# One ring of large slots, small products as row vectors, and the output projection moved to the end of a decode attention kernel

## The chip, the core and the metric

The kernel runs on one core of one Trainium2 chip. The metric is device time in microseconds. Three runs of the kernel before gave 1332.81, 1330.76 and 1330.81 us, a median of 1330.81 us. Beside these stands one profiled execution, which recorded every instruction, every DMA packet and the granted clock of the matrix engine. The engines are PE (matrix products), DVE (vector), ACT (scalar functions), POOL and SP; in this kernel SP issues nearly all DMAs.

## The reference

One token is decoded. The row x has 512 elements; its layer norm is xn. The result is x + attention(xn) + MLP(xn), all in float32.

```python
q = xn @ wq                         # [512] x [512, 4096]: 32 query heads of 128
s = q_h . k_cache[h // 4] * 128 ** -0.5     # 8 key/value heads, 65536 keys of 128 each
o = softmax(s) @ v_cache[h // 4]
attention = concat(o) @ wo          # [4096] x [4096, 512]
mlp = relu(xn @ w1) @ w2            # 512 -> 1792 -> 512
```

The keys and the values are 268 MB each. wq and wo are 8.4 MB each, w1 and w2 3.7 MB each. Nothing is read twice.

## The kernel before

**Staging.** All that is read comes through SP's DMA queue, in the order of the program. Keys and values use the pool `kv`: eight buffers of 16 KB per partition, one load of 2 MB each (4096 keys, `CHUNK`). The weights use a second pool, `wpool`, of four buffers of 8 KB per partition, one load of 1 MB each. A load is issued once the buffer that it takes has been released by the last instruction that read it.

**The loop.** For each of the eight key/value heads there are 16 key chunks, then `softmax(h)`, then 16 value chunks. `score_chunk` (L157) streams 512 keys at a time through PE against the four padded queries of the head, four matmuls side by side in the four 32-column tiles of the array (L166). DVE transposes the scores in 32x32 blocks (L171), ACT copies the four used columns (L173), DVE takes a maximum per chunk (L174). `softmax` (L180) finds the maximum over all partitions and lets ACT compute the exponentials (L197). `value_chunk` (L207) streams values through PE, again in four column tiles (L213). For heads 0 to 6 a matmul is 512 columns wide and holds four 128-key blocks at once (`WIDE`), of which only the matching columns are kept; for the last head it is 128 wide (`wide`, L202).

**The small products.** They are spread over the stream. `queries(h)` (L144) makes the queries of one head at its first key chunk: the weights are the stationary operand and xn, one column, is the moving one. `mlp_in(i)` (L262) does the same with a quarter of w1. `output(h)` (L242) runs at the second key chunk of the next head: it copies the accumulator, gathers the blocks (L252), and calls `project` (L234), which multiplies with that head's part of wo. `project` cuts the 512 output columns into four pieces of 128 and puts each on a column tile of its own (L236), all adding into `acc_y`. `mlp_out(i)` does the same with w2.

**The end.** The last value loads are cut into parts (`LAST`, L29: blocks of 8, 8, 8, 8 and 8, 8, 8, 4, 4), and after them come the last two blocks of w2 (L313). Then follow `output(7)`, `mlp_out(3)`, one addition (L319) and the store of the result (L320).

The matrix engine runs each float32 matmul as two instructions, so the counts on PE in the profile are twice those of the program.

Of the kernel before, what the change touches and what calls it, by code (L numbers as in the profile page):

```python
# [14 lines left out]
P = 128  # L15
# [14 lines left out]
WIDE = 4  # L30
A = D // P
FB = DFF // P
EPS = 1e-5
# [3 lines left out]
def attention_and_mlp_kernel(  # L37
# [30 lines left out]
    xT = const.tile([P, A], F32, name="xT")  # L68
    nc.scalar.dma_start(xT, x.rearrange("(p a) -> p a", p=P))
    x4 = const.tile([P, P], F32, name="x4")  # L70

    weights = {}

    def load(name, src):
        w = wpool.tile([P, 4, 512], F32, name="w")
        n, m = src.shape[1], src.shape[2]
        nc.sync.dma_start(w[:, :n, :m], src)
        weights[name] = w

    chunks = {}  # L80

    def load_k(h, n):
        t = kv.tile([P, CHUNK], F32, name="kv")
        nc.sync.dma_start(t, k[h, n])
        chunks["k", h, n] = t

    def load_v(h, n):
        t = kv.tile([P, CHUNK], F32, name="kv")
        src = v[h, n * CHUNK : (n + 1) * CHUNK, :].rearrange("(p b) d -> p (b d)", p=P)
        b = 0  # L90
        for nb in LAST.get(n, [NB]) if h == HKV - 1 else [NB]:
            cut = slice(b * DH, (b + nb) * DH)
            nc.sync.dma_start(t[:, cut], src[:, cut])
            b += nb
        chunks["v", h, n] = t

    load(("q", 0), wq[0])

# [5 lines left out]
    # sel[32 * c + 4 * b + g, b, g] = 1  # L104
# [5 lines left out]
    nc.vector.memset(x4, 0.0)  # L110
    qpad = [const.tile([P, 32], F32, name=f"qpad{i}") for i in range(2)]
    for t in qpad:
        nc.vector.memset(t, 0.0)
# [4 lines left out]
    nc.vector.memset(acc_y[:, :P], 0.0)  # L118

# [17 lines left out]
    # A Newton step: r * (1.5 - 0.5 * v * r * r).  # L137
# [6 lines left out]
    def queries(h):  # L144
        w = weights.pop(("q", h))
        pq = ps_m.tile([P, 512], F32, name="pm")
        for g in range(G):
            for a in range(A):
# [4 lines left out]
        nc.vector.tensor_copy(qpad[h % 2][:, :G], pq[:, :G])  # L153

    scores, chunk_max, probs, part_sum = {}, {}, {}, {}

    def score_chunk(h, n):  # L157
        t = chunks.pop(("k", h, n))
        if n == 0:
            scores[h] = work.tile([P, NCH * NB, G], F32, name="scores")  # L160
            chunk_max[h] = work.tile([P, G, NCH], F32, name="chunk_max")
        for s in range(TPC):
            pt = ps_s.tile([P, TW], F32, name="pt")
            for c in range(CT):
                lo = (s * CT + c) * TW
                nc.tensor.matmul(  # L166
                    pt[32 * c : 32 * c + 32, :], qpad[h % 2], t[:, lo : lo + TW],
                    start=True, stop=True,
                )
# [3 lines left out]
            nc.scalar.copy(scores[h][:, b0 : b0 + SUB, :], tr[:, :, :G])  # L173
        nc.vector.reduce_max(  # L174
            chunk_max[h][:, :, n],
            scores[h][:, n * NB : (n + 1) * NB, :].rearrange("p b g -> p g b"),
            axis=AX.X,
        )

    def softmax(h):  # L180
        m = work.tile([P, G], F32, name="m")
        nc.vector.reduce_max(m, chunk_max.pop(h), axis=AX.X)  # L182
# [10 lines left out]
        probs[h] = work.tile([P, NCH * NB, G], F32, name="probs")  # L193
        part_sum[h] = work.tile([P, G], F32, name="part_sum")
        s = scores.pop(h)
        for g in range(G):
            nc.scalar.activation(  # L197
                probs[h][:, :, g], s[:, :, g], AF.Exp, bias=bias[:, g : g + 1], scale=scale,
                accum_out=part_sum[h][:, g : g + 1],
            )  # L200

    def wide(h):  # L202
        """128-key blocks of one matmul: the columns of each meet the weights of all, and the
        block's own are kept. One for the last head, whose output is wanted soon."""
        return 1 if h == HKV - 1 else WIDE

    def value_chunk(h, n):  # L207
        t = chunks.pop(("v", h, n))
        w = wide(h)
        for i in range(NB // w):  # L210
            c = i % CT
            b = n * NB + i * w
            nc.tensor.matmul(  # L213
                acc_o[h % 2][32 * c : 32 * c + w * G, : w * DH],
                probs[h][:, b : b + w, :].rearrange("p b g -> p (b g)"),
                t[:, i * w * DH : (i + 1) * w * DH],
                start=(n == 0 and i < CT), stop=(n == NCH - 1 and i >= NB // w - CT),
            )

    norm = {}  # L220

    def totals(h):
        """1 / sum of a head's weights, in the places that gather its column tiles."""
        pm = ps_m.tile([P, 512], F32, name="pm")
        nc.tensor.matmul(pm[:, :G], ones, part_sum.pop(h), start=True, stop=True)  # L225
        r = work.tile([P, G], F32, name="r")
        nc.vector.reciprocal(r, pm[:, :G])  # L227
        norm[h] = work.tile([P, WIDE, G], F32, name="norm")
        for b in range(wide(h)):
            nc.vector.tensor_mul(norm[h][:, b, :], sel[:, b, :], r)  # L230
# [3 lines left out]
    def project(lhsT, row, last=False):  # L234
        for c in range(CT):
            nc.tensor.matmul(  # L236
                acc_y[32 * c : 32 * c + 1, :P], lhsT, row[:, c * P : (c + 1) * P],
                start=first[0], stop=last,
            )
        first[0] = False  # L240

    def output(h):  # L242
        probs.pop(h)
        n = wide(h)
        o = work.tile([P, WIDE, DH], F32, name="o")
        nc.vector.tensor_copy(  # L246
            o[:, :n, :].rearrange("p b d -> p (b d)"), acc_o[h % 2][:, : n * DH]
        )
        r = norm.pop(h)
        pm = ps_m.tile([P, 512], F32, name="pm")  # L250
        for b in range(n):
            nc.tensor.matmul(pm[:, :G], o[:, b, :], r[:, b, :], start=(b == 0), stop=(b == n - 1))  # L252
        oT = work.tile([P, G], F32, name="oT")
        nc.vector.tensor_copy(oT, pm[:, :G])  # L254
        w = weights.pop(("o", h))
        for g in range(G):
            project(oT[:, g : g + 1], w[:, g, :])

    hT = const.tile([P, FB], F32, name="hT")
    FQ = 4  # parts that the MLP's weights come in  # L260

    def mlp_in(i):  # L262
        w = weights.pop(("1", i))
        n = min(4, FB - 4 * i)
        pm = ps_m.tile([P, 512], F32, name="pm")
        for j in range(n):
            for a in range(A):
                nc.tensor.matmul(  # L268
                    pm[:, j : j + 1], w[:, a, j * P : (j + 1) * P], xn[:, a : a + 1],
                    start=(a == 0), stop=(a == A - 1),  # L270
                )
        nc.vector.tensor_scalar_max(hT[:, 4 * i : 4 * i + n], pm[:, :n], 0.0)

    def mlp_out(i):
        w = weights.pop(("2", i))
        for b in range(4 * i, min(4 * i + 4, FB)):
            project(hT[:, b : b + 1], w[:, b - 4 * i, :], last=(b == FB - 1))

# [1 line left out]
    for h in range(HKV):  # L280
        for n in range(NCH):
            load_k(h, n)
            if n == 0:
                queries(h)
            if n == 1:
                if h == 0:
# [63 lines left out]
```

## Time and profile before

| | |
|---|---|
| median of three runs | 1330.81 us (1330.76 to 1332.81) |
| span of the profiled execution | 1329.9 us |
| read from HBM | 560.99 MB, 422 GB/s over the span |
| PE busy | 795.2 us (60%) |
| DVE busy | 255.2 us (19%) |
| ACT busy | 103.5 us (8%) |
| keys in PE, L166 | 354.2 us in 2048 instructions |
| values in PE, L213 | 354.1 us in 2816 instructions |
| output and MLP projection, L236 | 14.5 us (with oT) |

The profiled execution is 0.9 us shorter than the median of the runs by its span; no other time of it is recorded. In the rows that are quoted below, a line such as `L166 PE MATMUL pt<-kv,qpad` reads: line 166 of the kernel, engine, operation, result and operands by the program's names. The two numbers after the bar are the busy time in us and the mean of one in ns; after the second bar stands the idle time of the engine before these instructions, and what ended most of it. "DMA share" is the busy share of the core's 16 DMA engines. A packet is the piece that one DMA engine moves as one; in this kernel it is one partition's row of a load.

### The profile page before, as it was taken

The numbers are of one execution on the slowest core, as the hardware profiler recorded it, in microseconds if no ns is written. First come the engines' busy times: TensorE is split into PE (matmuls) and PEld (weight loads), VectorE is DVE, ScalarE is ACT, GpSimd is POOL, SyncE is SP. The second block draws the span as 40 slices with busy tenths as digits, with TensorE's granted clock in tenths as the row PEclk, the third lists the DMA queues.
The fourth block names the chain that finished last, engine by engine and source line by source line (L and its number), as shares of the span: only waits on it lengthen the run. The fifth ranks groups of instructions, "written<-read, shape, count | busy, mean of one in ns | idle before, by whom it ended". The sixth has DMA issues, their size and how long they took to land.

```text
span 1329.9 us, 13199 instructions
## 1 busy us (share of the span) xinstructions
PE 795.2 (60%) x5702; PEld 241.1 (18%) x5702; DVE 255.2 (19%) x504; ACT 103.5 (8%) x323; POOL 0.7 (0%) x6
## 2 busy tenths in 40 slices
PE   5646757466555576655665456655666565665555
PEld 3211212112121121111211101111021110221233
DVE  3330023300233002330023300232003320033200
ACT  1020000200001000011000200002000120001100
POOL 0000000000000000000000000000000000000000
PEclk9777687777887767767777787776777867777777
DMA  9999999999999999999999999999999999999996
GB/s 394 427 429 426 427 423 428 428 426 428 425 428 427 427 427 426 426 427 427 427 429 427 428 427 428 426 429 429 426 427 429 425 429 428 426 428 428 426 426 274
DMA packets 43226, 561.86 MB, mean 422 GB/s; under 512 B 4760, under 2 KB 5280, under 8 KB 8224
## 3 DMA queue, kind: packets, MB, share of 16 engines
q1 hardware_dynamic: 43024, 561.01, 99.5%
q8 instruction: 45, 0.74, 0.2%
q14 instruction: 13, 0.11, 0.0%
q10 hardware_dynamic: 144, 0.00, 0.0%
HBM read 560.99 MB, written 0.00 MB: 422 GB/s over the span
## 4 chain that ended last, share of the span: by engine, by line
DMA 91%; PE 6%; ACT 2%; DVE 1%; issue 0%; SPq 0%; ACTq 0%
DMA kv<-k 47%; DMA kv<-v 41%; PE pt L166 3%; DMA w<-wo 3%; PE acc_o L213 2%; ACT probs L197 1%; PE acc_y L236 0%; DVE tr L171 0%; PE pm L225 0%; PE pm L252 0%; PE pm L190 0%; DVE chunk_max L174 0%; DVE mg L186 0%; PE pm L184 0%; ACT scores L173 0%
## 5 line engine op out<-in xcount | busy, mean ns | idle before, releaser
L166 PE MATMUL pt<-kv,qpad 128*32 128x512 f32 x2048 | 354.2, 823 | 240.5 <-DMA kv<-k 221.1
L213 PE MATMUL acc_o<-kv,probs 128*16 128x512 f32 (+1 forms) x2816 | 354.1, 655 | 209.1 <-DMA kv<-v 209.0
L171 DVE STREAM_TRANSPOSE tr<-pt 128x512 f32<-128x512 f32 x256 | 183.2, 716 | 347.2 <-PE pt L166 340.0
L166 PEld LDWEIGHTS pt<-kv,qpad 128*32 128x32 f32 x2048 | 78.5, 131 | 493.1 <-issue 282.8
L213 PEld LDWEIGHTS acc_o<-kv,probs 128*16 128x16 f32 (+1 forms) x2816 | 80.5, 110 | 462.9 <-DMA kv<-v 327.5
L173 ACT COPY scores<-tr 128x64 f32<-128x64 f32 x256 | 62.3, 243 | 1121.5 <-DVE tr L171 1121.5
L153 DVE COPY qpad<-pm 128x4 f32<-128x4 f32 x8 | 1.3, 162 | 376.4 <-PE pm L149 376.4
L174 DVE TENSOR_REDUCE chunk_max<-scores 128x4 f32<-128x128 f32 x128 | 48.5, 379 | 39.0 <-ACT scores L173 39.0
L246 DVE COPY o<-acc_o 128x512 f32<-128x512 f32 (+1 forms) x8 | 5.1, 642 | 225.7 <-PE acc_o L213 225.7
L149 PE MATMUL pm<-xn,w 128*128 128x1 f32 x256 | 40.0, 291 | 4.4 <-DMA w<-wq 2.6
L149 PEld LDWEIGHTS pm<-xn,w 128*128 128x128 f32 x256 | 39.5, 247 | 12.9 <-issue 11.1
L197 ACT ACTIVATE probs<-scores,bias 128x512 f32<-128x512 f32 x32 | 37.7, 1180 | 16.4 <-DVE bias L192 16.4
L225 PE MATMUL pm<-part_sum,ones 128*128 128x4 f32 x16 | 4.7, 365 | 42.4 <-ACT probs L197 42.4
L236 PE MATMUL acc_y<-w,oT 128*1 128x128 f32 x256 | 14.5, 331 | 2.0 <-DVE oT L254 2.0
L268 PEld LDWEIGHTS pm<-xn,w 128*128 128x128 f32 x112 | 14.5, 212 | 5.3 <-DMA w<-w 5.3
L268 PE MATMUL pm<-xn,w 128*128 128x1 f32 x112 | 14.9, 266 | 0.6 <-DMA w<-w 0.6
L252 PE MATMUL pm<-norm,o 128*128 128x4 f32 x58 | 8.8, 273 | 6.1 <-DVE o L246 6.1
L225 PEld LDWEIGHTS pm<-part_sum,ones 128*128 128x128 f32 x16 | 4.0, 312 | 43.1 <-ACT probs L197 43.1
L236 PEld LDWEIGHTS acc_y<-w,oT 128*1 128x1 f32 x256 | 9.3, 100 | 10.1 <-issue 5.6
L252 PEld LDWEIGHTS pm<-norm,o 128*128 128x128 f32 x58 | 8.1, 214 | 15.7 <-DVE o L246 15.7
L184 PE MATMUL pm<-ident,m 128*4 128x128 f32 x8 | 2.3, 284 | 14.3 <-DVE m L182 14.3
L227 DVE RECIPROCAL r<-pm 128x4 f32<-128x4 f32 x8 | 1.5, 183 | 45.9 <-PE pm L225 45.9
(47 smaller groups left out, 41.7 us busy)
## 6 DMA issues: line engine op xcount, KB each, us to landing
kv<-k SPq DMA_DIRECT2D x128, 2048.0 KB, 36.3
kv<-v SPq DMA_DIRECT2D x126, 2048.0 KB, 36.7
w<-wq SPq DMA_DIRECT2D x8, 1024.0 KB, 34.3
w<-wo SPq DMA_DIRECT2D x8, 1024.0 KB, 35.7
w<-w SPq DMA_DIRECT2D x6, 1024.0 KB, 36.7
kv<-v SPq DMA_DIRECT2D x7, 512.0 KB, 29.4
w<-w SPq DMA_DIRECT2D x1, 512.0 KB
kv<-v SPq DMA_DIRECT2D x2, 256.0 KB, 9.1
```

What stands on the lines that cost most here:

```text
L149: nc.tensor.matmul(pq[:, g : g + 1], w[:, a, g * DH : (g + 1) * DH], xn[:, a : a + 1], start=(a == 0), stop=(a == A - 1),)
L166: nc.tensor.matmul(pt[32 * c : 32 * c + 32, :], qpad[h % 2], t[:, lo : lo + TW], start=True, stop=True,)
L171: nc.vector.transpose(tr.rearrange("p b i -> p (b i)"), pt)
L173: nc.scalar.copy(scores[h][:, b0 : b0 + SUB, :], tr[:, :, :G])
L174: nc.vector.reduce_max(chunk_max[h][:, :, n], scores[h][:, n * NB : (n + 1) * NB, :].rearrange("p b g -> p g b"), axis=AX.X,)
L197: nc.scalar.activation(probs[h][:, :, g], s[:, :, g], AF.Exp, bias=bias[:, g : g + 1], scale=scale, accum_out=part_sum[h][:, g : g + 1],)
L213: nc.tensor.matmul(acc_o[h % 2][32 * c : 32 * c + w * G, : w * DH], probs[h][:, b : b + w, :].rearrange("p b g -> p (b g)"), t[:, i * w * ...
L225: nc.tensor.matmul(pm[:, :G], ones, part_sum.pop(h), start=True, stop=True)
L236: nc.tensor.matmul(acc_y[32 * c : 32 * c + 1, :P], lhsT, row[:, c * P : (c + 1) * P], start=first[0], stop=last,)
L246: nc.vector.tensor_copy(o[:, :n, :].rearrange("p b d -> p (b d)"), acc_o[h % 2][:, : n * DH])
L252: nc.tensor.matmul(pm[:, :G], o[:, b, :], r[:, b, :], start=(b == 0), stop=(b == n - 1))
L268: nc.tensor.matmul(pm[:, j : j + 1], w[:, a, j * P : (j + 1) * P], xn[:, a : a + 1], start=(a == 0), stop=(a == A - 1),)
```

## The change

There is now one pool, `ring`, of five slots of 32 KB per partition, for everything that is read. Key and value loads are 4 MB (8192 keys, 64 blocks of 128). wq is read first, in two loads of 4 MB, and the queries of all heads are made before the first key. w1 and w2 are read after the first head's values, one load each. wo is read last, after the last value, in parts of 8192, 4096, 2048, 1024, 512 and 512 columns, that is 4, 2, 1, 0.5, 0.25 and 0.25 MB.

The products with wq and w1 now have xn as the stationary operand, one column, and stream the weights, 512 columns at a time in four column tiles (`columns`); four transposes bring the row back onto partitions. `project` no longer uses four column tiles of 128 columns: it is one matmul of 512 columns into row 0 of `acc_y`. `output(h)` only gathers a head's output into `oT`; the 32 projections with wo, one per query head, all stand at the end behind `output(7)`. The last head's values use the 512-wide form as well, and its loads are no longer cut. The pool `work` has one buffer instead of two for most tiles.

```diff
-CHUNK = 4096  # keys of one load
+CHUNK = 8192
-LAST = {NCH - 2: [8, 8, 8, 8], NCH - 1: [8, 8, 8, 4, 4]}  # the blocks of the last loads, in parts
+LAST = [HALF * 2048, HALF * 2048 // 2, 2048, 1024, 512, 512]
...
-    kv = ctx.enter_context(tc.tile_pool(name="kv", bufs=8))
-    wpool = ctx.enter_context(tc.tile_pool(name="wpool", bufs=4))
-    work = ctx.enter_context(tc.tile_pool(name="work", bufs=2))
+    ring = ctx.enter_context(tc.tile_pool(name="ring", bufs=5))
+    work = ctx.enter_context(tc.tile_pool(name="work", bufs=1))
...
+    tq = [load_wq(i) for i in range(2)]
...
-    def queries(h):
...
+    def columns(weights, widths, relu=False):
+        pr = ps_m.tile([P, 512], F32, name="pm")
+        nc.vector.memset(pr, 0.0)
+        for a in range(A):
+            for c, n in enumerate(widths):
                 nc.tensor.matmul(
-                    pq[:, g : g + 1], w[:, a, g * DH : (g + 1) * DH], xn[:, a : a + 1],
+                    pr[32 * c : 32 * c + 1, :n], xn[:, a : a + 1], weights(c, a),
                     start=(a == 0), stop=(a == A - 1),
                 )
...
+        pt = ps_m.tile([P, 512], F32, name="pm")
+        for j in range(4):
+            nc.tensor.transpose(pt[:, j * P : (j + 1) * P], rows[:, j * P : (j + 1) * P], ident)
...
     def project(lhsT, row, last=False):
-        for c in range(CT):
-            nc.tensor.matmul(
-                acc_y[32 * c : 32 * c + 1, :P], lhsT, row[:, c * P : (c + 1) * P],
-                start=first[0], stop=last,
-            )
+        nc.tensor.matmul(acc_y[0:1, :], lhsT, row, start=first[0], stop=last)
...
+        if h == 0:
+            mlp(*load_mlp())
...
+    output(HKV - 1, norm)
+    for row, n, t in parts:
+        for f in range(row, row + n, D):
+            hg = f // D
+            project(oT[:, hg : hg + 1], t[:, f % ROW : f % ROW + D], last=(hg == HQ - 1))
-    y = const.tile([P, P], F32, name="y")
-    nc.vector.tensor_add(y, acc_y[:, :P], x4)
-    nc.sync.dma_start(out.rearrange("(c n) -> c n", c=CT), y[0:P:32, :])
+    y = const.tile([1, D], F32, name="y")
+    nc.vector.tensor_add(y, acc_y[0:1, :], x1)
+    nc.sync.dma_start(out.rearrange("(o n) -> o n", o=1), y)
```

In the built program PE executes, at the end, the last value matmuls, the four of `output(7)`, and then the 32 projections in the order of wo's parts.

More of the change, by code (lines that the diff above doesn't have):

```diff
@@ L69, in attention_and_mlp_kernel, with slot, load_wq @@
     nc.scalar.dma_start(xT, x.rearrange("(p a) -> p a", p=P))
[L70 to L80, printed above, removed]
+    x1 = const.tile([1, D], F32, name="x1")
+    def slot():
+        return ring.tile([P, ROW], F32, name="slot")
+    def load_wq(i):
+        t = slot()
+        nc.sync.dma_start(
+            t.rearrange("p (h f) -> p h f", h=HALF),
+            wq[i * HALF : (i + 1) * HALF].rearrange("h p a f -> p h (a f)"),
+        )
+        return t
     def load_k(h, n):
-        t = kv.tile([P, CHUNK], F32, name="kv")
+        t = slot()
         nc.sync.dma_start(t, k[h, n])
-        chunks["k", h, n] = t
+        return t
     def load_v(h, n):
-        t = kv.tile([P, CHUNK], F32, name="kv")
+        t = slot()
         src = v[h, n * CHUNK : (n + 1) * CHUNK, :].rearrange("(p b) d -> p (b d)", p=P)
[L90 to L97, printed above, removed]
+        nc.sync.dma_start(t, src)
+        return t
+    tq = [load_wq(i) for i in range(2)]
+    nc.scalar.dma_start(x1, x.rearrange("(o n) -> o n", o=1))
     ident = const.tile([P, P], F32, name="ident")
@@ L109, in attention_and_mlp_kernel @@
     nc.vector.tensor_add(sel, sel, places[3])
[L110 to L113, printed above, removed]
+    qall = const.tile([P, HKV, 32], F32, name="qall")
+    nc.vector.memset(qall, 0.0)
     acc_o = [ps_a.tile([P, 512], F32, name=f"acc_o{i}") for i in range(2)]
@@ L142, in attention_and_mlp_kernel, with score_chunk @@
     nc.vector.tensor_scalar_mul(xn, xc, st[:, 7:8])
-    def queries(h):
[L145 to L148, printed above, removed]
+    def columns(weights, widths, relu=False):
[3 more added lines that the diff above has]
+            for c, n in enumerate(widths):
                 nc.tensor.matmul(
-                    pq[:, g : g + 1], w[:, a, g * DH : (g + 1) * DH], xn[:, a : a + 1],
+                    pr[32 * c : 32 * c + 1, :n], xn[:, a : a + 1], weights(c, a),
                     start=(a == 0), stop=(a == A - 1),
                 )
[L153 to L161, printed above, removed]
+        rows = work.tile([P, 512], F32, name="rows")
+        if relu:
+            nc.vector.tensor_scalar_max(rows, pr, 0.0)
+        else:
+            nc.vector.tensor_copy(rows, pr)
+        pt = ps_m.tile([P, 512], F32, name="pm")
+        for j in range(4):
+            nc.tensor.transpose(pt[:, j * P : (j + 1) * P], rows[:, j * P : (j + 1) * P], ident)
+        return pt.rearrange("p (j c l) -> p c j l", j=4, c=CT)[:, :, :, 0]
+    for i, t in enumerate(tq):
+        w = t.rearrange("p (h a f) -> p h a f", h=HALF, a=A)
+        nc.vector.tensor_copy(
+            qall[:, i * HALF : (i + 1) * HALF, :G], columns(lambda c, a: w[:, c, a, :], [512] * 4)
+        )
+    scores = chunk_max = probs = part_sum = norm = None
+    def score_chunk(h, n, t):
         for s in range(TPC):
@@ L166, in score_chunk @@
                 nc.tensor.matmul(
-                    pt[32 * c : 32 * c + 32, :], qpad[h % 2], t[:, lo : lo + TW],
+                    pt[32 * c : 32 * c + 32, :], qall[:, h, :], t[:, lo : lo + TW],
                     start=True, stop=True,
@@ L192, in softmax @@
         nc.vector.tensor_copy(bias, pb[:, :G])
-        probs[h] = work.tile([P, NCH * NB, G], F32, name="probs")
-        part_sum[h] = work.tile([P, G], F32, name="part_sum")
-        s = scores.pop(h)
         for g in range(G):
             nc.scalar.activation(
-                probs[h][:, :, g], s[:, :, g], AF.Exp, bias=bias[:, g : g + 1], scale=scale,
-                accum_out=part_sum[h][:, g : g + 1],
-            )
[L202 to L210, printed above, removed]
+                probs[:, :, g], scores[:, :, g], AF.Exp, bias=bias[:, g : g + 1], scale=scale,
@@ L211, in value_chunk @@
+                accum_out=part_sum[:, g : g + 1],
+            )
+    def value_chunk(h, n, t):
+        for i in range(NB // WIDE):
             c = i % CT
-            b = n * NB + i * w
+            b = n * NB + i * WIDE
             nc.tensor.matmul(
[L214 to L217, printed above, removed]
-            )
@@ L220, in attention_and_mlp_kernel, with totals @@
-    norm = {}
-    def totals(h):
+                acc_o[h % 2][32 * c : 32 * c + WIDE * G, :],
+                probs[:, b : b + WIDE, :].rearrange("p b g -> p (b g)"),
+                t[:, i * 512 : (i + 1) * 512],
+                start=(n == 0 and i < CT), stop=(n == NCH - 1 and i >= NB // WIDE - CT),
+            )
+    def totals():
         pm = ps_m.tile([P, 512], F32, name="pm")
-        nc.tensor.matmul(pm[:, :G], ones, part_sum.pop(h), start=True, stop=True)
+        nc.tensor.matmul(pm[:, :G], ones, part_sum, start=True, stop=True)
@@ L226, in totals, with output @@
         r = work.tile([P, G], F32, name="r")
         nc.vector.reciprocal(r, pm[:, :G])
-        norm[h] = work.tile([P, WIDE, G], F32, name="norm")
-        for b in range(wide(h)):
-            nc.vector.tensor_mul(norm[h][:, b, :], sel[:, b, :], r)
+        t = work.tile([P, WIDE, G], F32, name="norm", bufs=2)
+        for b in range(WIDE):
+            nc.vector.tensor_mul(t[:, b, :], sel[:, b, :], r)
+        return t
+    oT = const.tile([P, HQ], F32, name="oT")
+    def output(h, norm):
+        o = work.tile([P, WIDE, DH], F32, name="o")
+        nc.vector.tensor_copy(o.rearrange("p b d -> p (b d)"), acc_o[h % 2])
+        pm = ps_m.tile([P, 512], F32, name="pm")
+        for b in range(WIDE):
+            nc.tensor.matmul(pm[:, :G], o[:, b, :], norm[:, b, :], start=(b == 0), stop=(b == WIDE - 1))
+        nc.vector.tensor_copy(oT[:, h * G : (h + 1) * G], pm[:, :G])
@@ L259, in attention_and_mlp_kernel @@
[L259 to L270, printed above, removed]
-                )
-        nc.vector.tensor_scalar_max(hT[:, 4 * i : 4 * i + n], pm[:, :n], 0.0)
@@ L316, in attention_and_mlp_kernel, with load_mlp @@
-    output(HKV - 1)
-    mlp_out(FQ - 1)
-    y = const.tile([P, P], F32, name="y")
-    nc.vector.tensor_add(y, acc_y[:, :P], x4)
-    nc.sync.dma_start(out.rearrange("(c n) -> c n", c=CT), y[0:P:32, :])
+        nc.tensor.matmul(acc_y[0:1, :], lhsT, row, start=first[0], stop=last)
+        first[0] = False
+    hT = const.tile([P, 4 * CT], F32, name="hT")
+    def load_mlp():
+        t1, t2 = slot(), slot()
+        nc.sync.dma_start(t1[:, : A * DFF], w1.rearrange("p a f -> p (a f)"))
+        nc.sync.dma_start(t2[:, : FB * D], w2.rearrange("p j n -> p (j n)"))
+        return t1, t2
@@ new lines, in mlp @@
+    def mlp(t1, t2):
+        w = t1[:, : A * DFF].rearrange("p (a f) -> p a f", a=A)
+        ends = [min(DFF, 512 * (c + 1)) for c in range(CT)]
+        nc.vector.tensor_copy(
+            hT.rearrange("p (c j) -> p c j", c=CT),
+            columns(
+                lambda c, a: w[:, a, 512 * c : ends[c]],
+                [ends[c] - 512 * c for c in range(CT)], relu=True,
+            ),
+        )
+        for j in range(FB):
+            project(hT[:, j : j + 1], t2[:, j * D : (j + 1) * D])
@@ new lines, in attention_and_mlp_kernel @@
+    for h in range(HKV):
+        scores = work.tile([P, NCH * NB, G], F32, name="scores")
+        chunk_max = work.tile([P, G, NCH], F32, name="chunk_max")
+        probs = work.tile([P, NCH * NB, G], F32, name="probs")
+        part_sum = work.tile([P, G], F32, name="part_sum")
+        for n in range(NCH):
+            t = load_k(h, n)
+            if n == 1 and h > 0:
+                output(h - 1, norm)
+            score_chunk(h, n, t)
+        softmax()
+        for n in range(NCH):
+            t = load_v(h, n)
+            if n == 0:
+                norm = totals()
+            value_chunk(h, n, t)
+        if h == 0:
+            mlp(*load_mlp())
@@ new lines, in attention_and_mlp_kernel @@
+    row, parts = 0, []
+    for n in LAST:
+        if (row * n) % ROW == 0 and row % ROW == 0:
+            t = slot()
+        parts.append((row, n, t))
+        while n:
+            h, f = divmod(row, 2048)
+            m = min(n, 2048 - f)
+            if n >= 2048 and f == 0:
+                m = n - n % 2048
+                nc.sync.dma_start(
+                    t[:, row % ROW : row % ROW + m].rearrange("p (h f) -> p h f", f=2048),
+                    wo[h : h + m // 2048].rearrange("h p g f -> p h (g f)"),
+                )
+            else:
+                nc.sync.dma_start(
+                    t[:, row % ROW : row % ROW + m], wo[h].rearrange("p g f -> p (g f)")[:, f : f + m]
+                )
+            row += m
+            n -= m
```

66 lines of the change are left out of this document (7 added, 59 removed).

## The prediction

> **What bounds the kernel now.** I read the page first: engines, slices, DMA, the chain.
>
> ```profile
> span 1329.9 us, 13199 instructions
> PE 795.2 (60%) x5702; PEld 241.1 (18%) x5702; DVE 255.2 (19%) x504; ACT 103.5 (8%) x323; POOL 0.7 (0%) x6
> ...
> DMA  9999999999999999999999999999999999999996
> GB/s 394 427 429 426 427 423 428 428 426 428 425 428 427 427 427 426 426 427 427 427 429 427 428 427 428 426 429 429 426 427 429 425 429 428 426 428 428 426 426 274
> ...
> HBM read 560.99 MB, written 0.00 MB: 422 GB/s over the span
> ...
> DMA 91%; PE 6%; ACT 2%; DVE 1%; issue 0%; SPq 0%; ACTq 0%
> ...
> L246 DVE COPY o<-acc_o 128x512 f32<-128x512 f32 (+1 forms) x8 | 5.1, 642 | 225.7 <-PE acc_o L213 225.7
> ```
>
> The DMA engines are busy in every slice but the last, at about 427 GB/s, while PE is busy 60%: the kernel is as long as its reading, plus the start and the end. All bytes are still read once, so only three things can move the time: how fast the bytes come, what precedes the first, and what follows the last. The timeline of the end, and the DMA view of 1320 to 1323 us (40 slices of 75 ns):
>
> ```profile
> 1320.88 1.90 PE L213 MATMUL acc_o<-kv,probs 128*4 128x128 f32 x32 [0.65 <-DMA kv<-v]
> ...
> 1322.86 0.29 DVE L246 COPY o<-acc_o 128x128 f32<-128x128 f32 x1 [70.73 <-PE acc_o L213]
> ...
> 1324.04 1.89 PE L236 MATMUL acc_y<-w,oT 128*1 128x128 f32 x32 [0.26 <-DVE oT L254]
> ...
> 1325.70 1.08 PE L236 MATMUL acc_y<-w,hT 128*1 128x128 f32 x16
> 1326.85 0.29 DVE L319 TENSOR_TENSOR y<-acc_y,x 128x128 f32<-128x128 f32 x1 [2.86 <-PE acc_y L236]
> 1327.17 0.60 SPq L320 DMA_DIRECT2D y<-y  x1
> ```
>
> ```profile
> GB/s 191 219 218 137 219 218 191 219 218 218 191 164 164 191 219 191 219 218 191 191 164 164 137 109 109 55 109 109 109 109 109 109 109 109 109 82 82 82 27 0
> ```
>
> The last byte lands at 1322.9 us, and 7.0 us follow it, of which the store takes 2.7 (1327.17 to 1329.9). The small remaining projections take 2.8 us.
>
> **Part 1: larger packets.** The DMA view of a stretch with 16 KB packets only, and of one with a load of w1, whose rows are 2 KB:
>
> ```profile
> DMA packets 2348, 34.23 MB, mean 428 GB/s; under 512 B 259, under 2 KB 259, under 8 KB 259
> ...
> q1 hardware_dynamic: 2346, 34.19, 100.5%
> ```
>
> ```profile
> DMA packets 626, 2.39 MB, mean 399 GB/s; under 512 B 32, under 2 KB 32, under 8 KB 544
> ...
> q1 hardware_dynamic: 626, 2.39, 99.8%
> ```
>
> The first is 840 to 920 us. Without the 259 tiny packets, 2087 packets of 16 KB use 80 us x 16 engines x 1.005, that is 0.616 us each. The second is 28.5 to 34.5 us: 512 packets of 2 KB and 82 of 16 KB use 6 x 16 x 0.998 = 95.8 us; less 82 x 0.616, a 2 KB packet takes 0.0885. Eight of them are 0.708 against 0.616, so a packet costs (0.708 - 0.616) / 7 = 0.013 us beside its bytes. A share above 100% says that packets of an engine overlap a little; I take off 0.5% of 0.616, which leaves 0.010 us. If a 32 KB row is one packet, the 128 key and value loads have 16384 packets fewer: 16384 x 0.010 / 16 engines = 10.2 us. w1 and w2 have 2048 + 640 packets by the code before and 256 rows of 28 KB after, some 2430 fewer, 1.5 us. Together -11.7 us. The bounds: 0 if a row is still moved 16 KB at a time (the trace shows no longer packet), -15 at 0.013; a loss has no row for it, since the rate only rises with the row. I take the fitted value, the nearest. The last byte then lands at 1311.2.
>
> **Part 2: the projection at the end.** This part sets the sign. After the last value byte come 8.4 MB of wo, 20 us. In this time PE does the last value chunk (16 matmuls, at most 7.3 us by the rows below) and `output(7)` (1.2 us from the copy at 1322.86 to the projections at 1324.04, some 0.4 more with a wide copy). That is over before the first 4 MB of wo have landed, which is 10 us before the last byte (4.2 MB at 427 GB/s, 9.8 us). From there 32 projections of 512 columns follow, each two instructions, all on one column tile. Their price is read from the timeline at two granted clocks, with the weight loads of each group of four tiles:
>
> ```profile
> 39.27 3.64 PE L166 MATMUL pt<-kv,qpad 128*32 128x512 f32 x16 [1.43 <-DMA kv<-k]
> 40.09 0.23 PEld L166 LDWEIGHTS pt<-kv,qpad 128*32 128x32 f32 x4 [0.62 <-issue]
> 40.94 0.23 PEld L166 LDWEIGHTS pt<-kv,qpad 128*32 128x32 f32 x4 [0.62 <-issue]
> ...
> 49.06 1.92 PE L166 MATMUL pt<-kv,qpad 128*32 128x512 f32 x16 [1.29 <-DMA kv<-k]
> 49.49 0.15 PEld L166 LDWEIGHTS pt<-kv,qpad 128*32 128x32 f32 x4 [0.27 <-DVE chunk_max L174]
> 49.92 0.16 PEld L166 LDWEIGHTS pt<-kv,qpad 128*32 128x32 f32 x4 [0.27 <-issue]
> ```
>
> ```profile
> 39.20:43.00 3.80, 3.64 (x16) 0.69 (x16) 0.75 (x2) 0.24 (x1) 0.00 (x0) 0.50 0.99 423
> 49.00:51.00 2.00, 1.92 (x16) 0.50 (x16) 0.96 (x2) 0.07 (x1) 0.00 (x0) 1.00 0.96 410
> 1320.80:1329.90 9.10, 5.23 (x82) 2.84 (x82) 0.74 (x3) 0.00 (x0) 0.00 (x0) 0.50 0.09 34
> ```
>
> The column after POOL is the granted clock. At 1.00 a group of four follows the other by 0.43 us, at 0.50 by 0.85: exactly the ratio of the clocks. Weights load meanwhile, so they cost nothing. In such a group each tile streams its own 512 columns, so I price a lone matmul of 512 columns like the whole group: 0.43 us an instruction. So four tiles in company do four times the work of one alone, and a single tile gives that up: 32 x 2 x 0.427 = 27.3 us at full clock, where four tiles of 128 would need 6.8. The bounds are 0.107 us an instruction (tiles share one stream; 6.8 us in all) and 0.85 (half clock; 54.6 us). The last row shows that PE ends at clock 0.50 before, although it worked 5.2 of 9.1 us; and from 39.2 on it stayed at 0.50 through 3.6 us of dense work. I take 4.2 us at half clock before it rises, 2.1 us more (an estimate, somewhat over those 3.6).
>
> The Trainium skill (TensorE: Matmul & The Clock Gate, Part 3) measures 3.07 times the speed of one tile for four row tiles, not 4. By that a lone instruction would take 0.33 us, the projections 21.0, and the sum below would be 6.3 less, 1329. The groups show a full 512 columns per tile and clock, so I stay with the row.
>
> The end, counted from the last byte: start -10.0; 27.3 + 2.1 of projections; 0.2 until DVE starts; 0.7 for an addition now 512 wide (L246's mean, 642 ns, on as many columns); 2.7 for the store. That is +23.0 against +7.0 before: +16.0 us. The wait that ends last is no longer for a DMA but for PE, which works through landed slots.
>
> **Part 3: what is hidden.** The first keys, in the timeline:
>
> ```profile
> 17.28 6.83 PE L166 MATMUL pt<-kv,qpad 128*32 128x512 f32 x48 [0.26 <-DVE qpad L153]
> ```
>
> A slot of 4 MB takes 9.8 us to arrive and at most 2 x 3.64 = 7.3 us of PE, so slots come free in time, and five slots hold 49 us of reading against eight buffers of 4.9 us before. What hides all small work is this queue:
> - wq first: the keys' first matmul moves from 17.3 us (row above) to some 31, when key chunk 0 lands after 12.6 MB. The first wq slot is free at about 19 us, and the queue is filled to 49. Cost 0; without that cover it would be some 14 us.
> - w1 and w2: `columns` takes 16 matmuls (7 us at half clock), a copy like L246's and four transposes, the 14 projections of w2 12 to 24 us. This delays the next head's keys by up to 24 us after w2 has landed, and four slots of 9.8 us stand behind it. Cost 0.
> - `softmax` and single buffers in `work`: the chain is the same, and scores, exponentials and values of one head already follow each other on PE. Cost 0. The gathering of `output(h)` now stands ahead of the next keys, about 2 us of PE waiting on DVE, inside the 2.5 us of slack per slot. Cost 0.
> - SP issues some 140 loads instead of 280; each waits for a slot, and nothing but loads stands behind it. Cost 0.
> - The start: the first load is issued as before. Cost 0.
>
> **The sum.** 1329.9 - 11.7 + 16.0 = 1334.2 for the profiled execution. Its span is 0.9 below the median of the runs, so 1330.8 + 4.3 = 1335.1 us: slower by 0.3%, just over the 0.2% (2.7 us) that a measurement of this kernel can tell from no change.
>
> **The rivals.**
> - *The clock doesn't rise at the end.* One tile of four and one column of 32 may not count as work for what grants the clock. Then the projections take 54.6 us in place of 29.4: 1360. For it: the clock of 0.50 in the last row. Against it: with PE working only in stretches of 2 to 4 us, the clock was 0.50 at 39.2 and 1.00 at 49.0 us, and here are 27 us without a pause. The Trainium skill (TensorE: Matmul & The Clock Gate, Part 1) has the clock doubled after some 3.4 us of sustained work and says nothing of lone tiles; by it this rival falls and 1335 stands.
> - *A lone tile streams faster than one of four* (ends on the other side). If an instruction took half, 0.213 us, the projections would end 13.6 us earlier: 1321, faster. It decides from 4.3 / 64 = 0.067 us less, at 0.36 us an instruction. For it: no row shows a lone tile. Against it: the groups scale exactly with the clock, not with shared reading. A milder form, company costing a tile a quarter of its speed (0.33 us an instruction, 21 us in all), ends at 1329, no change.
> - *Packets stay at 16 KB*, so part 1 doesn't do what it says: 10.2 us more, 1345. For it: no longer packet in the trace. Against it: none is asked for there.
>
> **How the numbers follow.** The forecast, 1331 to 1341 (gain of part 1 from 5 to 15, cold clock from 0 to 4 us): 0.55, of which 0.10 lies within 0.2%. Clock stays low: 0.20. Lone tile faster: 0.15, of which 0.05 at 1329. Packets of 16 KB: 0.10. So faster 0.11 (0.10 of the lone tile, 0.01 of the forecast), same 0.15, slower 0.74. To leave out no more than 0.2 the range must take in the low clock: 1328 to 1361.
>
> **What would show it.** Right: GB/s in the middle slices near 430; packets of 32 KB, half as many; the last byte near 1311; 64 instructions on the projection's line spaced 0.43 us, from about 1301 to 1331, at clock 1.00 after some 4 us; the chain ending in PE, not DMA. Wrong: 427 GB/s in the middle (part 1), spacing of 0.85 or 0.21 us (part 2), idle DMA near 180 to 220 us, where the MLP now stands (part 3).

## The result, and the profile after

The changed kernel takes 1336.63 us (median of four runs, 1336.1 to 1337.29) against 1331.13 us for the kernel before on the same chip (the three runs above and a fourth, 1331.46 us): 1.0041 times as long, with a 95% interval of 1.0026 to 1.0055. It is slower by 5.5 us. The profiled execution has a span of 1334.3 us, 4.4 more than before.

The page of the kernel after, in the parts that answer to those shown of before:

```profile
span 1334.3 us, 10207 instructions
PE 788.5 (59%) x4404; PEld 192.4 (14%) x4404; DVE 248.7 (19%) x437; ACT 103.5 (8%) x323; POOL 0.7 (0%) x6
...
GB/s 393 440 424 439 424 435 429 431 431 426 436 428 434 430 429 435 427 434 429 427 433 430 431 433 428 434 427 435 428 430 434 425 438 424 438 425 431 433 419 84
DMA packets 21344, 561.64 MB, mean 421 GB/s; under 512 B 2354, under 2 KB 2354, under 8 KB 2740
...
DMA 81%; PE 16%; ACT 2%; DVE 1%; issue 0%; SPq 0%; DVEq 0%; ACTq 0%
DMA slot<-k 50%; DMA slot<-v 27%; PE pt L177 7%; PE acc_o L216 6%; DMA slot<-wo 3%; PE acc_y L247 2%; ACT probs L205 2%; DVE tr L182 0%; DVE chunk_max L185 0%; PE pm L226 0%; PE pm L201 0%; DVE mg L197 0%; PE pm L195 0%; ACT scores L184 0%; DVE dg L199 0%
...
L247 PE MATMUL acc_y<-slot,oT 128*1 128x512 f32 x64 | 29.2, 619 | 3.1 <-DMA slot<-wo 3.1
```

The middle slices move about 431 GB/s in place of 427, with half the packets. The last slice moves 84 GB/s in place of 274: the reading ends early, and something else fills the rest. PE is no busier over the whole span (59%). Its share of the chain that ended last rose from 6 to 16%, but that alone says little of the end: the projection (L247) has only 2% of it, and the key and value matmuls (L177, L216) have 13%. The sign is that the projection's line is busy for 29.2 us in one piece. The timeline of the end:

```profile
1292.23 5.01 PE L216 MATMUL acc_o<-slot,probs 128*16 128x512 f32 x32 [3.30 <-DMA slot<-v]
...
1299.16 0.16 DVE L242 COPY oT<-pm 128x4 f32<-128x4 f32 x1 [1.15 <-PE pm L241]
...
1302.18 29.17 PE L247 MATMUL acc_y<-slot,oT 128*1 128x512 f32 x64 [3.06 <-DMA slot<-wo]
1302.99 0.13 PEld L247 LDWEIGHTS acc_y<-slot,oT 128*1 128x1 f32 x1 [0.72 <-issue]
1303.84 0.13 PEld L247 LDWEIGHTS acc_y<-slot,oT 128*1 128x1 f32 x1 [0.72 <-issue]
...
1305.87 0.08 PEld L247 LDWEIGHTS acc_y<-slot,oT 128*1 128x1 f32 x1 [0.34 <-issue]
1306.30 0.09 PEld L247 LDWEIGHTS acc_y<-slot,oT 128*1 128x1 f32 x1 [0.34 <-issue]
...
1331.39 0.68 DVE L318 TENSOR_TENSOR y<-acc_y,x 1x512 f32<-1x512 f32 x1 [32.07 <-PE acc_y L247]
1332.10 0.33 SPq L319 DMA_DIRECT2D y<-y  x1
```

PE waits until 1302.18 for the first 4 MB of wo, and then works through 64 instructions without a pause, first 0.85 and then 0.43 us apart. The stretches show why (the column after POOL is the granted clock), and the DMA view of 1305 to 1320 us (40 slices of 0.375 us) shows when the reading ended:

```profile
1302.20:1305.40 3.20, 3.20 (x4) 0.45 (x5) 0.00 (x0) 0.00 (x0) 0.00 (x0) 0.51 0.89 362
1305.50:1331.30 25.80, 25.80 (x61) 4.91 (x59) 0.00 (x0) 0.00 (x0) 0.00 (x0) 1.00 0.11 42
```

```profile
GB/s 339 306 213 197 208 284 219 202 240 224 191 197 197 158 33 55 49 38 0 0 0 0 0 0 0 0 0 0 0 0 0 0 0 0 0 0 0 0 0 0
```

The clock rose after 3.2 us of lone-tile work. The last byte landed at 1311.7. So the kernel has both at once: 11.2 us less reading than before (1322.9 to 1311.7), and 22.6 us behind the last byte in place of 7.0.

### The profile page after: what moved, and what is told of

The parts are those of the page before. It is cut to its first block, busy times and chain, and to the rows that moved or that the text cites. A ratio compares the mean times of both kernels' runs of the same rounds, so it can differ in the third digit from the quotient of the medians.

```text
span 1334.3 us, 10207 instructions
## 1 busy us (share of the span) xinstructions
PE 788.5 (59%) x4404; PEld 192.4 (14%) x4404; DVE 248.7 (19%) x437; ACT 103.5 (8%) x323; POOL 0.7 (0%) x6
## 2 busy tenths in 40 slices
DMA packets 21344, 561.64 MB, mean 421 GB/s; under 512 B 2354, under 2 KB 2354, under 8 KB 2740
## 4 chain that ended last, share of the span: by engine, by line
DMA 81%; PE 16%; ACT 2%; DVE 1%; issue 0%; SPq 0%; DVEq 0%; ACTq 0%
DMA slot<-k 50%; DMA slot<-v 27%; PE pt L177 7%; PE acc_o L216 6%; DMA slot<-wo 3%; PE acc_y L247 2%; ACT probs L205 2%; DVE tr L182 0%; DVE chunk_max L185 0%; PE pm L226 0%; PE pm L201 0%; DVE mg L197 0%; PE pm L195 0%; ACT scores L184 0%; DVE dg L199 0%
## 5 line engine op out<-in xcount | busy, mean ns | idle before, releaser
L177 PE MATMUL pt<-slot,qall 128*32 128x512 f32 x2048 | 361.3, 868 | 243.4 <-DMA slot<-k 243.4
L216 PE MATMUL acc_o<-slot,probs 128*16 128x512 f32 x2048 | 347.4, 844 | 206.8 <-DMA slot<-v 206.8
L177 PEld LDWEIGHTS pt<-slot,qall 128*32 128x32 f32 x2048 | 95.5, 151 | 502.5 <-issue 496.5
L216 PEld LDWEIGHTS acc_o<-slot,probs 128*16 128x16 f32 x2048 | 68.2, 125 | 478.4 <-DMA slot<-v 257.2
L238 DVE COPY o<-acc_o 128x512 f32<-128x512 f32 x8 | 5.5, 692 | 549.1 <-PE acc_o L216 549.1
L185 DVE TENSOR_REDUCE chunk_max<-scores 128x4 f32<-128x256 f32 x64 | 38.5, 602 | 19.8 <-ACT scores L184 19.8
L205 ACT ACTIVATE probs<-scores,bias 128x512 f32<-128x512 f32 x32 | 37.7, 1184 | 18.2 <-DVE bias L203 18.2
L247 PE MATMUL acc_y<-slot,oT 128*1 128x512 f32 x64 | 29.2, 619 | 3.1 <-DMA slot<-wo 3.1
L150 PE MATMUL pm<-slot,xn 128*1 128x512 f32 (+1 forms) x96 | 17.8, 888 | 12.7 <-DMA slot<-wq 10.4
L247 PE MATMUL acc_y<-slot,hT 128*1 128x512 f32 x28 | 12.2, 592 | 0.9 <-DMA slot<-w 0.9
L247 PEld LDWEIGHTS acc_y<-slot,oT 128*1 128x1 f32 x64 | 5.4, 86 | 25.9 <-issue 22.8
```

The costliest lines, as they stand in the source:

```text
L150: nc.tensor.matmul(pr[32 * c : 32 * c + 1, :n], xn[:, a : a + 1], weights(c, a), start=(a == 0), stop=(a == A - 1),)
L177: nc.tensor.matmul(pt[32 * c : 32 * c + 32, :], qall[:, h, :], t[:, lo : lo + TW], start=True, stop=True,)
L185: nc.vector.reduce_max(chunk_max[:, :, n], scores[:, n * NB : (n + 1) * NB, :].rearrange("p b g -> p g b"), axis=AX.X,)
L205: nc.scalar.activation(probs[:, :, g], scores[:, :, g], AF.Exp, bias=bias[:, g : g + 1], scale=scale, accum_out=part_sum[:, g : g + 1],)
L216: nc.tensor.matmul(acc_o[h % 2][32 * c : 32 * c + WIDE * G, :], probs[:, b : b + WIDE, :].rearrange("p b g -> p (b g)"), t[:, i * 512 : (i ...
L238: nc.vector.tensor_copy(o.rearrange("p b d -> p (b d)"), acc_o[h % 2])
```

## The experiments

The theory: larger packets save some 11 us, and the projection on one column tile, which nothing covers at the end, costs some 16. Each part can be had without the other. All runs are compared with the 1336.6 us of the changed kernel or with the kernel before, which was run again beside each group of them and took 1330.8 to 1331.5 us; the groups ran on different chips.

**Four tiles, nothing else.** The changed kernel with the old form of the projection (the addition and the store go back to four rows with it):

```diff
-        nc.tensor.matmul(acc_y[0:1, :], lhsT, row, start=first[0], stop=last)
+        for c in range(4):
+            nc.tensor.matmul(
+                acc_y[32 * c : 32 * c + 1, :128], lhsT, row[:, c * 128 : (c + 1) * 128],
+                start=first[0], stop=last,
+            )
```

> The changed kernel with the old form of the projection: four matmuls of 128 columns on four column tiles, nothing else. My theory (a lone column tile gives up a factor of four, and the end waits for PE): the 32 projections need 6.8 us at full clock in place of 29.2, so they keep up with the landing of wo and end within 0.5 us of the last byte at 1311.7. Behind it 0.2 + 0.3 (a narrower addition) + 2.7 us: a span of about 1315.3, 19 us less than the 1334.3 of the changed kernel; 1318 by the clock of the runs, 1.0% faster than the kernel before. Rival (the end is held by the landing of wo's parts or by the clock at half speed, not by the form of the matmul): less than 5 us gained, 1332 or more.

Measured: 1318.48 us (1318.3 to 1318.88), 0.9904 times the kernel before (0.9887 to 0.9920); a span of 1316.8. Its timeline at the end:

```profile
1302.38 8.55 PE L250 MATMUL acc_y<-slot,oT 128*1 128x128 f32 x224 [2.78 <-DMA slot<-wo]
...
1311.23 0.96 PE L250 MATMUL acc_y<-slot,oT 128*1 128x128 f32 x21 [0.31 <-DMA slot<-wo]
...
1313.19 0.60 PE L250 MATMUL acc_y<-slot,oT 128*1 128x128 f32 x11 [1.00 <-issue]
...
1313.83 0.29 DVE L324 TENSOR_TENSOR y<-acc_y,x 128x128 f32<-128x128 f32 x1 [14.03 <-PE acc_y L250]
```

Of the 32 projections, 28 (224 instructions) are done in 8.55 us, and PE waits for wo's last parts again. This form alone gives back 18.2 us. It beats both kernels, by 1.4% and 1.0%. The span is 1.5 us over the expected one; 1.0 of that is the idle time before 1313.19. The row names no wait for it, but the packed trace has the last semaphore increment of a wo load at 1312.8 us, inside this time, so most of it looks like a wait for the last part. The clock was slow for longer here than in the changed kernel:

```profile
1302.40:1307.00 4.60, 4.60 (x88) 3.15 (x92) 0.00 (x0) 0.00 (x0) 0.00 (x0) 0.50 0.79 321
```

**Two tiles.** The same with two matmuls of 256 columns, on two column tiles:

```diff
-        nc.tensor.matmul(acc_y[0:1, :], lhsT, row, start=first[0], stop=last)
+        for c in range(2):
+            nc.tensor.matmul(
+                acc_y[64 * c : 64 * c + 1, :256], lhsT, row[:, c * 256 : (c + 1) * 256],
+                start=first[0], stop=last,
+            )
```

> The changed kernel with the projection cut into two matmuls of 256 columns on two column tiles. If the cost is that of columns per tile, the projections take 13.7 us at full clock and 1.7 for the cold start: from 1302.2 to 1317.5, then 0.2 + 0.4 + 2.7; a span of 1320.9, 13.4 less than the changed kernel, 1323 by the runs. If tiles in company slow each other (3.07 for four), two would gain less than half: 1325 or more.

Measured: 1323.34 us (1322.99 to 1323.8), a span of 1321.2. In its timeline the projection is one row:

```profile
1302.37 15.67 PE L250 MATMUL acc_y<-slot,oT 128*1 128x256 f32 x128 [2.75 <-DMA slot<-wo]
```

15.67 us on two tiles, 29.17 on one; without the slow first stretch (some 1.6 us in each) it is 14.1 against 27.6, half. So two tiles in company are not slower than one alone, and the price that was read from groups of four was not too high for a lone tile.

**Half of the lone-tile work under cover.** The form stays, but the first 4 MB of wo are read before the last head's values, and their 16 projections stand there:

```diff
         softmax()
+        if h == HKV - 1:
+            early = slot()
+            nc.sync.dma_start(
+                early.rearrange("p (h f) -> p h f", f=2048),
+                wo[0:HALF].rearrange("h p g f -> p h (g f)"),
+            )
...
+            if h == HKV - 1 and n == 1:
+                for hg in range(HALF * G):
+                    project(oT[:, hg : hg + 1], early[:, hg * D : (hg + 1) * D])
...
-    row, parts = 0, []
-    for n in LAST:
+    row, parts = HALF * 2048, []
+    for n in LAST[1:]:
```

> The changed kernel with the lone-tile projection as it is, but the first half of wo (4 MB) is read before the last head's values and its 16 projections stand there, under the reading; 16 are left for the end. My theory (the loss is work on a lone tile that nothing covers): 16 projections from the landing of the next 2 MB, 4.9 us before the last byte at 1311.7, that is 1306.8 + 13.7 + 1.7 for the cold start + 0.2 + 0.7 + 2.7: a span of 1325.8, 8.5 us less than the changed kernel, 1328 by the runs. Rival (the end is set by the landing and the store, or the 16 early ones are not hidden): 1334 or more.

Measured: 1328.03 us (ten runs, 1326.96 to 1328.49), a span of 1326.1; 0.9978 times the kernel before (0.9968 to 0.9987). Two rows of its timeline, one for the early and one for the late work:

```profile
1228.52 14.35 PE L247 MATMUL acc_y<-slot,oT 128*1 128x512 f32 x29
...
1310.11 13.04 PE L247 MATMUL acc_y<-slot,oT 128*1 128x512 f32 x30
```

The line of the DMA view of 1220 to 1260 us, around the early work:

```profile
DMA packets 636, 17.29 MB, mean 432 GB/s; under 512 B 65, under 2 KB 65, under 8 KB 65
```

The same 14 us cost nothing at 1228, where the reading went on at 432 GB/s, while at 1310 most of it lies bare behind the last byte. So the place matters as much as the form. That the slow form is free was seen here and in the MLP of the changed kernel; other places were not tried. The 1328 us were met partly by luck: the late projections began at 1308.1 in place of 1306.8 us, because PE was still busy with the last values, and the 1.7 us of slow clock were not paid, because the clock had risen at 1307.1 under those values.

**Rows of 16 and of 8 KB.** The changed kernel, each key and value load in two or in four DMAs:

```diff
-        nc.sync.dma_start(t, k[h, n])
+        for i in range(2):
+            nc.sync.dma_start(t[:, i * 4096 : (i + 1) * 4096], k[h, n][:, i * 4096 : (i + 1) * 4096])
...
-        nc.sync.dma_start(t, src)
+        for i in range(2):
+            nc.sync.dma_start(t[:, i * 4096 : (i + 1) * 4096], src[:, i * 4096 : (i + 1) * 4096])
```

> The changed kernel with each key and value load cut in two DMAs with rows of 16 KB in place of 32 KB; slots, order and compute unchanged. My theory (a packet costs 0.010 us beside its bytes): 16384 packets more, 10.2 us more of reading, 427 GB/s in the middle in place of 431, a span of 1344.5 and 1347 by the runs. Rival (the shorter reading came from the small weights, from fewer loads or from the ring): at most 1.5 us more, 1338.

> The changed kernel with each key and value load cut in four DMAs with rows of 8 KB. If the cost is one of each packet (0.010 us, as 16 KB rows gave 10.6 us in all): 49152 packets more than with 32 KB, 31 us, 418 GB/s in the middle and 1368 by the runs. If it were a cost of rows above 16 KB or of the number of loads alone, under 1358.

Measured: 1347.28 us (1346.98 to 1348.49) and 1369.13 us (two runs, 1368.41 and 1369.84). The line of packets in the DMA view of 840 to 920 us, for the changed kernel, for 16 KB and for 8 KB:

```profile
DMA packets 1187, 34.45 MB, mean 431 GB/s; under 512 B 134, under 2 KB 134, under 8 KB 134
```

```profile
DMA packets 2339, 34.09 MB, mean 426 GB/s; under 512 B 258, under 2 KB 258, under 8 KB 258
```

```profile
DMA packets 4610, 33.56 MB, mean 420 GB/s; under 512 B 515, under 2 KB 515, under 8 KB 515
```

The first extra 16384 packets cost 10.65 us, all 49152 cost 32.5: 0.0104 and 0.0106 us a packet on its engine (times 16, divided by the packets). The cost is one of each packet from 8 to 32 KB. These kernels also issue more DMAs, 128 packets in each, so by themselves they don't separate a cost of the DMA from that of its packets. The changed kernel's own timeline does so in one place: the first part of wo is 4 MB in one DMA with rows of 8 KB, 512 packets. It landed 9.95 us after the last values (1292.23 to 1302.18), which is 422 GB/s, close to the 420 of 8 KB rows with 128 packets a DMA and not to the 431 of 32 KB rows. So in this stretch the cost goes with the packets.

**Large loads alone.** The kernel before with loads of 4 MB in four slots, its projections and places kept:

```diff
-CHUNK = 4096  # keys of one load
+CHUNK = 8192  # keys of one load
-LAST = {NCH - 2: [8, 8, 8, 8], NCH - 1: [8, 8, 8, 4, 4]}
+LAST = {NCH - 1: [32, 8, 8, 8, 4, 4]}
-    kv = ctx.enter_context(tc.tile_pool(name="kv", bufs=8))
+    kv = ctx.enter_context(tc.tile_pool(name="kv", bufs=4))
```

(The chunk numbers at which the small work stands are halved with it.)

> The kernel before with part 1 alone: key and value loads of 4 MB with rows of 32 KB in four slots, the weights' pool and the projections as they were, the small work at the same places in the stream, the last head's last load cut into parts of 32, 8, 8, 8, 4 and 4 blocks. My theory: 10.2 us less reading and the same end: a span near 1319.5, 1321 by the runs, 0.8% faster than the kernel before. Rival (the gain needs the ring of five slots, or four slots run dry): 1327 to 1331.

Measured: 1320.49 us (1320.36 to 1320.89), 0.9920 times the kernel before (0.9905 to 0.9935), 11.0 us less, with no ring and no new order. Not all of that is reading. The throughput of 1311 to 1314 us (40 slices of 75 ns), and the stretch of the end as it was shown of the kernel before:

```profile
GB/s 218 219 191 191 164 219 191 218 218 218 410 109 164 82 82 82 82 82 82 82 55 82 82 55 55 82 82 82 82 82 55 27 0 0 0 0 0 0 0 0
```

```profile
1311.30:1318.60 7.30, 3.33 (x90) 1.99 (x82) 0.74 (x3) 0.00 (x0) 0.00 (x0) 0.97 0.10 36
```

The last byte lands at 1313.4, 9.5 us sooner than before, a little under the 10.2 that were expected. Behind it stand 5.1 us in place of 7.0, as PE does much the same end at clock 0.97 in place of 0.50 (busy for 3.3 us in place of 5.2): these 1.9 us were not in the expectation, and they are why the total is above 10.2. The four-tile kernel is 2.0 us faster than this one, and its last byte lands 1.5 us sooner. That is the size of the term for longer w1 and w2 rows, which was not tested alone. So the rest of the change (ring, order, row vectors), taken together, is worth little either way.

**Fewer slots.** The changed kernel with a ring of three, and of two:

```diff
-    ring = ctx.enter_context(tc.tile_pool(name="ring", bufs=5))
+    ring = ctx.enter_context(tc.tile_pool(name="ring", bufs=3))
```

> The changed kernel with a ring of three slots in place of five, nothing else. By part 3 of the prediction a slot is used up in at most 7.3 us of the 9.8 that the next takes to land. With three slots, after the softmax the value slot 0 is free about 22 us after the last key slot landed, and the slot that waits for it is wanted at 29; the MLP's second slot is held for some 22 us behind its landing, less than two slots of 9.8 and the one in flight: no stall above 3 us for each of these places, 1337 to 1342. Rival (the depth of five is what hides the small work): 10 us or more for the eight softmaxes and the MLP, 1350 or more.

> The changed kernel with a ring of two slots. Here the cover is gone by my count: at each softmax the load behind the next one waits until about 22 us after the last key slot landed, while the slot before it is full at 20; with the 2 us from issue to first data some 4 to 5 us for each of eight heads, and as much at the MLP and at wq: 1337 + 40 to 60, 1375 to 1400. If the steady stretches stall as well (a slot's release comes too late for the next load), 64 pairs of slots add 1 us or more each: over 1430.

Measured: 1337.13 us (1336.43 to 1337.48) with three, no different from five; 1413.61 us with two (1410.99 and 1416.23). The throughput for two slots in the DMA views of 205 to 225 us, where the MLP stands, and of 300 to 320 us, behind a softmax (40 slices of 0.5 us each):

```profile
GB/s 590 393 328 655 131 590 459 262 721 66 721 328 459 524 197 590 328 66 66 66 0 0 0 0 0 0 0 0 0 0 0 0 590 393 66 0 721 328 262 786
```

```profile
GB/s 524 393 328 459 393 524 262 459 393 410 524 262 655 262 393 524 393 524 393 328 524 393 524 328 197 0 0 0 0 33 786 131 66 66 786 197 655 393 0 852
```

So the small work is hidden with three slots already, and five are cover that nothing here uses. With two, the reading stops where the count said, some 3 us behind this softmax and 7 at the MLP (slices at or near 0). The loss is 77 us, between the two cases of the expectation (40 to 60, and over 90). Eight softmaxes and the MLP at these sizes make little over 30. A stretch without either, 240 to 300 us, shows that the steady reading loses as well:

```profile
DMA packets 852, 24.74 MB, mean 412 GB/s; under 512 B 96, under 2 KB 96, under 8 KB 96
```

The changed kernel has 434 GB/s in the same stretch. How the loss is made up can be read from the queue's line on the two pages, first with five slots, then with two:

```profile
q1 hardware_dynamic: 21154, 561.00, 98.0%
```

```profile
q1 hardware_dynamic: 21154, 561.00, 95.2%
```

The packets took 0.980 x 1334.3 = 1307.6 us of all engines with five slots and 0.952 x 1409.2 = 1341.6 with two, for the same number of packets and the same bytes. So of the 75 us between the two spans, 41 are engines without work, within the 40 to 60 of the count, and 34 are packets that took longer, which the count didn't have. Why a packet takes longer with two slots isn't shown.

**An uneven end.** The four-tile kernel with one part of wo (2 MB) loaded as 16 DMAs of eight partitions:

```diff
+                step = 8 if n == ROW // 2 else P
+                for p0 in range(0, P, step):
+                    nc.sync.dma_start(
+                        t[p0 : p0 + step, row % ROW : row % ROW + m].rearrange("p (h f) -> p h f", f=2048),
+                        wo[h : h + m // 2048, p0 : p0 + step].rearrange("h p g f -> p h (g f)"),
+                    )
```

> The four-tile kernel with one part of wo (2 MB) loaded as 16 DMAs of eight partitions each, in place of one of 128. In the runs so far only some 9 of the 16 DMA engines are busy in the last 7 us (share 0.59): each engine has the same bytes and some are 0.5% slower. If a load of eight partitions goes to eight engines only, and these are mostly the ones that end early, the last byte comes some 2 to 3 us sooner than 1312 and the run takes about 1316; if they are mostly the late ones, it comes 4 to 5 us later, 1323; if the load is spread over all 16 in any case, nothing changes (1318 to 1319). This tells nothing of the two parts of the change; it asks whether the uneven end can be used.

Measured: 1336.17 us (1333.32 to 1337.5), 18 us more than with one DMA of 128 partitions, and outside all three cases. In its timeline SP is the reason that shows:

```profile
1306.40 11.69 SPq L310 DMA_DIRECT2D slot<-wo  x10
```

Ten issues took 11.7 us, when all 16 engines would move the whole 2 MB in 5. Why an issue took 1.17 us here isn't shown. Whether the engines that end late can be given less work stays open.

## Why the prediction was right, point by point

- **Part 1** put the saving at 11.7 us and the last byte at 1311.2 us; the trace has 1311.7, a saving of 11.2. The price of a packet, 0.010 us, fitted from one stretch with rows of 2 KB, was measured as 0.0104 to 0.0106 over whole runs, and rows of 32 KB are moved as one packet: 21344 packets in place of 43226. This was shown from both sides (16 KB rows in the kernel after, 32 KB rows in the kernel before, the latter with 9.5 us by the last byte). The rival in which packets stay at 16 KB falls.
- **Part 2** put 29.4 us on the projections and 23.0 us behind the last byte; the trace has 29.2 and 22.6. The price of a lone tile, read from groups of four, held: 0.43 us an instruction at full clock. So the rival of a faster lone tile falls, and with it the milder form at 1329, since two column tiles halve the time. The small terms were each a little off: the start, 10.0 us before the last byte, was 9.5; the store took 2.2 us (1332.10 to 1334.3), not 2.7; the slow clock lasted 3.2 us, not 4.2. That last one isn't a fixed cost: it was 4.6 us or more in the four-tile kernel. The Trainium skill (TensorE: Matmul & The Clock Gate, Part 3) has 3.07 times the speed of one tile for four row tiles, and the estimate of 1329 was worked out from it. The traces here, with column tiles, don't agree: a group of four takes as long as a lone tile (0.43 us), and two give twice the speed of one.
- **The clock rival** falls by the stretch at 1305.5: one column on one tile is work enough. The Trainium skill (TensorE: Matmul & The Clock Gate, Part 1) has the rise after about 3.4 us of sustained work. The trace of the kernel after agrees, with 3.2; that of the four-tile kernel has 4.6 or more.
- **Part 3**, everything hidden, held: three slots do as well as five, and the middle slices show no dip where the MLP stands. Its reason, the count of 49 us of queued reading, was far more than is needed.
- **The sum**, 1334.2 for the profiled execution, met a span of 1334.3. That it is this close is luck: the last byte came 0.5 us late, and the end behind it was 0.4 us shorter. By the runs 1335.1 was said and 1336.6 measured, because the median lies 2.3 us above the profiled span here, where the 0.9 of the kernel before was taken as fixed. It isn't: every run whose span is recorded, whatever its kernel, took 1.7 to 2.1 us longer than its own span, so the two figures say only how the profiled execution lay to the median, and a forecast from it carries an error of about this size.

## What to carry to other kernels

When a kernel is as long as its reading, count two things alone: what the bytes cost, packet by packet, and what runs after the last of them. Work that is free in the stream is paid in full at the end, so the form of the matmul must be chosen for the place where it stands: four column tiles where nothing covers it, while a slower form can do where enough loaded data stands behind it. Test the two halves of such a change apart; here one was worth -11 us and the other +16, and the sum was a loss of 0.4%.

## What the runs showed of the hardware

The 16 DMA engines do not end together. Every large load is made of equal rows, 128 or a multiple, and the semaphore that announces it is raised 16 times as it lands. For the first part of wo the packed trace of the kernel after has the first of these at 1294.3 us and the last at 1302.1, right before PE began at 1302.18: one load lands over 7.8 us. One stretch of the kernel after, with the DMA share and the GB/s as the last two columns:

```profile
1304.00:1310.00 6.00, 6.00 (x14) 1.06 (x12) 0.00 (x0) 0.00 (x0) 0.00 (x0) 0.89 0.59 239
```

The share is 0.59: on the average the engines were idle for 41% of this time, while data came until 1311.7. The kernel before shows the same from 1320 us on, where the throughput falls in steps. The idle share of this stretch alone is 0.41 x 6 = 2.5 us of reading on all engines. Why some are behind is open (which engine moved which packet isn't recorded), and the one attempt to use it lost 18 us.
